# Where the transposes of a banded attention stand among the matrix products of a gated layer

## The chip, the cores and the metric

The kernel runs on one core of a Trainium2 chip. The metric is the device time of one execution in microseconds (us). The engines of a core work side by side, each through its own queue in order: TensorE (PE in the profile, with its weight loads as PEld), VectorE (DVE), ScalarE (ACT), GpSimd (POOL), and SyncE (SP), which issues the DMAs. They wait for each other by semaphores.

## The reference

```python
# q, k, v: (8, 8, 576, 64); window 32, dilation 4; heads 0-3 plain, heads 4-7 dilated
scores = scale * np.matmul(q, k.transpose(0, 1, 3, 2))
scores = np.where(masks, scores, -1000000000.0)      # 32 keys of each query are left
scores = scores - np.max(scores, axis=-1, keepdims=True)
attn = np.exp(scores)
attn = attn / (np.sum(attn, axis=-1, keepdims=True) + 1e-09)
x = np.matmul(attn, v)                               # then (4608 tokens, 512)
...
xn = x / rms * rms_g
g = xn @ w_gate
silu = g * (1.0 / (1.0 + np.exp(-g)))
val = xn @ w_val
out = silu * val @ w_out                             # (4608, 512), d_ff = 1536
```

## The kernel before, in words

**Units.** The 4608 tokens are worked on in 16 units of 288 tokens. A unit has two parts. The *attention* of a unit is 14 small pieces, called bursts here (burst 0 to burst 13): each is one block of queries against its band of keys, for two heads at once. The *layer* of a unit is the product with the gate weights, with the value weights and with the output weights, in 12 slices j of 128 of the 1536 columns. While TensorE works through the layer of one unit, the attention of the next unit is slipped in between; units are named here by their attention, so "unit 7" is the attention that runs beside the layer of unit 6.

**Ticks.** The order is written out by hand. The main loop (L747 to L775) goes through ticks, three for each slice j: in the gate tick `gate` runs the 12 products into PSUM tile `g` (L588 to L590: each 32-bit product is made of three products of split parts), in the value tick `val` runs 12 products into tile `v`, and in the output tick `proj` adds 12 products of an earlier slice into the four `acc` tiles. After the products of a tick, `attend` (L713) puts the attention steps of this tick behind them: the transposes of one burst, the output product of another, the scores of a third, in this order (L457). `plan` (L706) says at which ticks: a burst has its scores at tick q, its transposes five ticks later (L726), its output product eight ticks later. From the third unit's attention on the scores come every second tick, so that scores and output product share a tick, and the transposes stand in the ticks between.

**A burst, step by step.** Scores (L455) go to PSUM tile `s`. One tick later `scores_max` (L332, L337, DVE) takes them out, two ticks later `scores_exp` (L347, ACT) makes exponentials, four ticks later `scores_norm` (L350) sums and inverts on DVE (L354, L355) and multiplies on POOL, once for each of the two heads (L357). Then TensorE transposes the two 96 x 128 blocks of `t` into spare columns of a PSUM bank (L429), one tick later `untranspose` copies them out in two parts on ACT (L412) and DVE (L414), and the output product (L443, L444) reads these.

**Spare columns.** Tiles `g` and `v` have one bank of 512 columns each and use 288; the transposes get the next 192. `free` says whose: in the gate tick the gate's, in the value tick again the gate's (`g_free`, filled one tick earlier), in the output tick the value's (`v_free`). A tile is guarded as a whole: an instruction that writes spare columns waits for the readers of the 288 that stand ahead of it, and a reader waits for the writers ahead of it. The gate's readers are the hyperbolic tangent on ACT (L622) and `silu` on DVE (L627), both issued one tick after the gate tick; the value's reader is `prod` on DVE (L640), issued one tick after the value tick, which puts the slice's result together. Its split (L651 ACT, L652 POOL) is read three ticks later by `proj`.

**Order within a tick.** What other engines do in a tick is put off by `later` and written out by `flush` at the tick's start, in the order of a rank: `scores_norm` has -1, `prod` 0, `untranspose` 0.2, the copy of the output product (L377) 0.5, `scores_max` 0.7, `silu` 0.8, exponentials 2, the addition L387 4, the splits of q and k 3 to 5 (L315 on DVE, L306 on POOL).

Of the kernel before, what the change touches and what calls it, by code (L numbers as in the profile page):

```python
# [49 lines left out]
def geometry(u, c):  # L50


    half = u % 2
    if c < NC // 2:
        if half:
            return [(QB * i, QB * i, 0, P) for i in range(U // QB)], QB, U + W
        return [(QB * i, max(QB * i - W, 0), 0 if i else W, P if i else QB)
                for i in range(U // QB)], QB, U
    nq = U // DIL
    keys = nq + (W if half else 0)  # L60
    return [(nq * r, keys * r, 0 if half else W, keys) for r in range(DIL)], nq, keys * DIL
# [3 lines left out]
def attn_moe(ctx: ExitStack, tc: tile.TileContext, qk_in, v_in, w_gate, w_val, w_out, rms_g, outT):  # L65
# [41 lines left out]
    def later(dt, rank, fn):  # L107
        put_off.setdefault(now[0] + dt, []).append((rank, fn))

    def flush():  # L110
        for _, fn in sorted(put_off.pop(now[0], []), key=lambda e: e[0]):
            fn()
# [61 lines left out]
    def decode(k):  # L174

        for _ in range(k):
            later(0, 5, step)
# [20 lines left out]
    def split_weight(kind, j, e):  # L198
        n = pieces.index((kind, j))
        m, k = divmod(n, 2)  # L200

        tag = f"hi{n if n % 4 == 3 and n < 2 * NP - 4 else n - n % 4}"
        if tag not in his:
            parts = 1 if n % 4 == 3 and n < 2 * NP - 4 else 3 if n < 2 * NP - 4 else 4
            his[tag] = cst.tile([P, parts, NC, P], F32R, tag=tag, name=f"{tag}_{kind}{j}")
        hi = his[tag][:, 0 if tag == f"hi{n}" else n % 4]
        if k == 0:
            los[m] = cst.tile([P, 2, NC, P], F32R, tag=f"slot{state['free']}", name=f"lo_{m}")
        else:
            state["free"] = m  # L210
        lo = los[m][:, k]
        wts[kind, j] = hi, lo
        A.copy(out=hi, in_=single(kind, j))
        e.tensor_tensor(out=lo, in0=single(kind, j), in1=hi, op=ALU.subtract)
# [186 lines left out]
    def bursts(u):  # L401
        return [(u, c, i) for c in range(NC) for i in range(len(geometry(u, c)[0]))]
# [206 lines left out]
    def gate(u, j):  # L609
        g_ps = group("g", u, j)  # L610
        if u == 0:
            used.append(("g", j))
        g = g_ps[:, :U]

        def tanh():
            nonlocal g
            t = (sb.tile([P, U], F32, tag="hhi", name=f"h_{j}", bufs=2) if u == 0 else
                 sb.tile([P, U], F32, tag="th", name=f"th_{u}_{j}", bufs=1))
            if u + j == 0:
                g = sb.tile([P, U], F32, tag="hhi", name="g_first", bufs=2)  # L620
                V.tensor_tensor(out=g, in0=g_ps[:, :U], in1=root[0], op=ALU.mult)
            A.activation(out=t, in_=g, func=AF.Tanh, scale=0.5)  # L622
            gv[u, j] = t

        def silu():
            t = gv[u, j]
            V.scalar_tensor_tensor(out=t, in0=t, scalar=1.0, in1=g, op0=ALU.add, op1=ALU.mult)  # L627

        later(1, 0 if u + j else 0.65, tanh)
        later(1, 0.8, silu)  # L630
        return g_ps[:, U:U + 2 * QB]

    def val(u, j):
        v_ps = group("v", u, j)
        if u == 0:
            used.append(("v", j))

        def prod():
            t = gv[u, j]
            V.tensor_tensor(out=t, in0=t, in1=v_ps[:, :U], op=ALU.mult)  # L640
            if u + j == 0:
                V.tensor_tensor(out=t, in0=t, in1=root[0], op=ALU.mult)

        def parts():
            t = gv.pop((u, j))
            if u == 0:
                hs[u, j] = t
                return
            hi = sb.tile([P, U], F32R, tag="hhi", name=f"hhi_{u}_{j}", bufs=2)
            lo = late[0].tile([P, U], F32R, tag="hlo", name=f"hlo_{u}_{j}", bufs=2)  # L650
            A.copy(out=hi, in_=t)  # L651
            G.tensor_tensor(out=lo, in0=t, in1=hi, op=ALU.subtract)  # L652
            hs[u, j] = (hi, lo)

        later(1 if u + j else 2, 0, prod)
        later(1 if u + j else 2, 0.5, parts)
        return v_ps[:, U:U + 2 * QB]

    def proj(u, j):
        if u == 0:  # L660
            used.append(("o", j))
        h = hs.pop((u, j))
        for d in range(NC):
            if j == 0:
                acc[u, d] = ps.tile([P, 512], F32, tag=f"acc{d}", name=f"acc_{u}_{d}")[:, :U]
            three(acc[u, d], weight("o", u, j), d, h, j == 0, j == NJ - 1)
            if j == NJ - 1:
                later(1, 0.7, lambda d=d: give(u, d))
# [35 lines left out]
    events = {}  # L704

    def plan(u, base, q_at, t_at, o_at):  # L706
        for b, *ts in zip(bursts(u), q_at, t_at, o_at):
            for kind, t in zip("qto", ts):
                events.setdefault(base + t, {})[kind] = b
        events.setdefault(base + o_at[-1] + 3, {})["sum"] = u  # L710
        events.setdefault(base + o_at[-1] + (5 if u else 4), {})["apply"] = u

    def attend(t_ps, **tags):  # L713
        e = events.pop(now[0], {})
        if any(k in e for k in "qto"):
            products(e.get("q"), e.get("t"), e.get("o"), t_ps, **tags)
        if "sum" in e:
            rms_sum(e["sum"])
        if "apply" in e:
            rms_apply(e["apply"])  # L720

    ends = nb + LAG + OUT + 5
    plan(0, 0, range(nb), range(LAG, nb + LAG), range(LAG + OUT, nb + LAG + OUT))
    for u in range(1, NU):
        q_at = [LAST - (LAST - EARLY[u > NNAT]) * (nb - 1 - k) // (nb - 1) for k in range(nb)]
        t_at, o_at = [t + 5 for t in q_at], [t + 8 for t in q_at]  # L726
        if u < NNAT:
            q_at = (-1, 1, 2, 4, 5, 7, 8, 10, 11, 13, 14, 16, 17, 19)
            t_at, o_at = [t + 5 for t in q_at], [t + 7 for t in q_at]
        plan(u, ends - 2 + 3 * NJ * (u - 1), q_at, t_at, o_at)  # L730
    for n in range(ends):
# [10 lines left out]
        if n == ends - 1:  # L742
            _, v_free = gate(0, 0), val(0, 0)
# [3 lines left out]
    for u in range(NU):  # L747
        for j in range(NJ):
            for part in range(0 if u + j else 2, 3):
                t = 3 * (u * NJ + j) + part  # L750
                if used and (t % 3 != 2 if t >= SPLITS else t % 2 == 0):
                    later(0, 6, lambda: split_weight(*used.pop(0), V if t >= SPLITS else G))
                if u == 0:
                    decode(2 if t < 6 else 1 + t % 2 if len(ops) > 3 else int(t > 30))
                opening = len(ops) <= 3
                flush()
                if opening and not late:
                    early.close()
                    late.append(ctx.enter_context(tc.tile_pool(name="late", bufs=2)))
                if part == 0:  # L760
                    free = gate(u, j)
                elif part == 1:
                    free = val(u, j)
                else:
                    if prev is not None:
                        proj(*prev)
                    prev = (u, j)
                    free = v_free
                if part == 1:
                    g_free, v_free = g_free, free  # L770
                    free = g_free
                elif part == 0:
                    g_free = free
                attend(free)
                now[0] += 1  # L775
    flush()
# [69 lines left out]
```

## Time and profile before

| | us |
|---|---|
| median of three runs | 1160.24 (1160.02 to 1163.11) |
| the profiled execution's own time | 1162.36 |
| its span in the trace | 1160.6 |
| TensorE busy in the span | 1125.2 (97%) |
| VectorE, ScalarE, GpSimd busy | 798.8, 716.1, 611.5 |

The profiled execution lies 2.1 us above the median, and 1.8 us of it lie outside the traced span. In the trace a matmul's record is longer than the step to the next one, since matmuls are pipelined: the step from one 288-column product to the next is 0.13 us, the record 0.29 us. How late a matmul came is therefore read from start to start. The first 141 us hold the attention and the layer of the first unit, in another form (L585, L452, L438), and the stretch from 141 to 209 us the second unit's layer; after that each unit takes 67.5 us until the last, whose layer has no attention beside it.

### The profile page before, as it was taken

The page shows a single profiled execution, that of the slowest core. Times are in us where ns is not written, and L with a number is a line of the kernel's source. Part 1 is how long each engine was busy: PE and PEld are TensorE (multiplying, and loading weights), DVE is VectorE, ACT ScalarE, POOL GpSimd, SP SyncE. Part 2 cuts the span into 40 slices and gives each one's busy share as a digit, 9 for nine tenths or more (in the row PEclk, how much of TensorE's full clock was granted, in tenths as well). Part 3 has the DMA queues.
Part 4 walks back from the last instruction along what each step waited for, and adds up shares of the span by engine and source line. Part 5 has one row for each costly group of instructions (what it writes and reads, how often), then busy time and mean ns, then how long its engine had stood idle before and what let it go on. Part 6 is the DMA issues. An engine that isn't in the chain of part 4 may idle for free.

```text
span 1160.6 us, 25964 instructions
## 1 busy us (share of the span) xinstructions
PE 1125.2 (97%) x8357; PEld 1088.5 (94%) x8357; DVE 798.8 (69%) x2898; ACT 716.1 (62%) x2605; POOL 611.5 (53%) x1087
## 2 busy tenths in 40 slices
PE   8799788999999999999999999999999999999998
PEld 7577588999999999999999999999999999999998
DVE  5899777866758676675858767585776758586421
ACT  7476376675757567575666757576665757666311
POOL 6365344565546556564555655465565645565211
PEclk9899899999999999999999999999999999999999
DMA  8555221221213122131312213131221313120000
GB/s 245 156 210 179 76 75 39 80 61 31 82 37 103 39 70 62 35 86 34 95 41 81 58 31 90 31 101 40 71 61 35 95 33 91 38 81 15 1 21 22
DMA packets 61545, 82.19 MB, mean 71 GB/s; under 512 B 7298, under 2 KB 41090, under 8 KB 61410
## 3 DMA queue, kind: packets, MB, share of 16 engines
q1 hardware_dynamic: 61410, 80.54, 23.2%
q8 instruction: 67, 1.10, 0.4%
q14 instruction: 68, 0.56, 0.2%
HBM read 71.08 MB, written 9.44 MB: 69 GB/s over the span
## 4 chain that ended last, share of the span: by engine, by line
PE 75%; DVE 18%; issue 3%; ACT 2%; DMA 1%; POOL 0%; SPq 0%; POOLq 0%; DVEq 0%; ACTq 0%
PE acc L588 8%; PE acc L589 7%; PE acc L590 7%; PE g L588 7%; PE v L588 7%; PE g L590 7%; PE g L589 7%; PE v L589 7%; PE v L590 7%; DVE qs L315 3%; PE s L455 3%; PE o L443 3%; DVE t L337 2%; DVE xraw L551 2%; PE g L429 2%
## 5 line engine op out<-in xcount | busy, mean ns | idle before, releaser
L652 POOL TENSOR_TENSOR hlo<-th,hhi 128x288 fp32r<-128x288 f32 x180 | 144.8, 805 | 200.7 <-ACT hhi L651 196.9
L357 POOL TENSOR_SCALAR t<-t,sum 72x104 f32<-72x104 f32 (+3 forms) x442 | 165.7, 386 | 113.6 <-DVE sum L355 97.7
L590 PE MATMUL acc<-hhi,lo 128*128 128x288 f32 x720 | 212.1, 295 | 0.0
L590 PE MATMUL g<-xhi,lo 128*128 128x288 f32 x612 | 181.0, 296 | 0.0
L590 PE MATMUL v<-xhi,lo 128*128 128x288 f32 x612 | 180.3, 295 | 0.0
L651 ACT CAST hhi<-th 128x288 fp32r<-128x288 f32 x180 | 78.0, 433 | 163.7 <-DVE th L640 159.9
L347 ACT ACTIVATE t<-t,sum 96x128 f32<-96x128 f32 (+3 forms) x448 | 166.8, 375 | 12.3 <-DVE sum L337 11.4
L276 POOL TENSOR_TENSOR vlo<-vt,vhi 128x128 fp32r<-128x128 f32 x196 | 93.5, 477 | 122.7 <-ACT vhi L272 103.0
L387 DVE TENSOR_TENSOR xraw<-o,xraw 64x96 f32<-64x96 f32 (+1 forms) x392 | 106.8, 272 | 61.2 <-ACT xraw L377 56.4
L622 ACT ACTIVATE th<-g 128x288 f32<-128x288 f32 x180 | 73.8, 410 | 121.4 <-PE g L590 93.4
L590 PEld LDWEIGHTS acc<-hhi,lo 128*128 128x128 f32 x720 | 135.3, 188 | 0.0
L332 DVE TENSOR_TENSOR t<-s,mask 96x256 f32<-96x256 f32 (+3 forms) x196 | 71.7, 366 | 81.0 <-PE s L455 61.8
L627 DVE SCALAR_TENSOR_TENSOR th<-th,g 128x288 f32<-128x288 f32 x180 | 80.4, 447 | 68.0 <-ACT th L622 68.0
L590 PEld LDWEIGHTS g<-xhi,lo 128*128 128x128 f32 x612 | 115.5, 189 | 0.0
L590 PEld LDWEIGHTS v<-xhi,lo 128*128 128x128 f32 x612 | 115.1, 188 | 0.0
L588 PE MATMUL g<-xhi,hi_g 128*128 128x288 f32 x357 | 111.4, 312 | 0.6 <-DVE pt L414 0.5
L377 ACT COPY xraw<-o 64x96 f32<-64x96 f32 (+1 forms) x392 | 101.0, 258 | 16.1 <-PE o L444 13.8
L588 PE MATMUL acc<-hhi,hi_o 128*128 128x288 f32 x360 | 110.3, 306 | 0.0
L306 POOL TENSOR_TENSOR ks<-qk,ks 128x288 fp32r<-128x288 f32 (+2 forms) x112 | 107.4, 973 | 3.4 <-ACT ks L301 3.4
L589 PE MATMUL acc<-hlo,hi_o 128*128 128x288 f32 x360 | 106.6, 296 | 0.0
L640 DVE TENSOR_TENSOR th<-th,v 128x288 f32<-128x288 f32 x180 | 81.4, 452 | 36.2 <-PE v L590 33.2
L589 PE MATMUL g<-xlo,hi_g 128*128 128x288 f32 x322 | 95.4, 296 | 0.0
(173 smaller groups left out, 3569.7 us busy)
## 6 DMA issues: line engine op xcount, KB each, us to landing
qk<-in_qk_dram SPq DMA_DIRECT2D x60, 288.0 KB, 2.8
vt<-in_v_dram SPq DMA_DIRECT2D x196, 64.0 KB, 1.9
qk<-in_qk_dram SPq DMA_DIRECT2D x30, 352.0 KB, 3.0
out_dram<-ot SPq DMA_DIRECT2D x64, 144.0 KB, 1.9
qk<-in_qk_dram SPq DMA_DIRECT2D x30, 304.0 KB, 2.8
raw<-in_w_gate_dram SPq DMA_DIRECT2D x12, 512.0 KB, 4.3
raw<-in_w_val_dram SPq DMA_DIRECT2D x12, 512.0 KB, 4.0
raw<-in_w_out_dram SPq DMA_DIRECT2D x12, 512.0 KB, 4.2
```

The lines of the kernel that those rows point to most:

```text
L276: G.tensor_tensor(out=vl, in0=vs.pop(b), in1=vh, op=ALU.subtract)
L306: ek.tensor_tensor(out=ks[:, 1, :nkt], in0=kr, in1=ks[:, 0, :nkt], op=ALU.subtract)
L347: A.activation(out=t[:nq, a, :n], in_=t[:nq, a, :n], func=AF.Exp, scale=-1.0, bias=sm[:nq, a, 0:1], accum_out=sm[:nq, a, 1:2])
L357: (V if u == 0 and (c, i) > (NC - 1, 0) else G).tensor_scalar(out=t[:nq, a, :n], in0=t[:nq, a, :n], scalar1=sm[:nq, a, 3:4], scalar2=1.0, ...
L377: A.copy(out=to[a * D:(a + 1) * D], in_=o[a * D:(a + 1) * D, (2 + a) * nq:(3 + a) * nq])
L387: V.tensor_tensor(out=to[rows], in0=o[rows, a * nq:(a + 1) * nq], in1=to[rows], op=ALU.add)
L588: PE.matmul(out, wh[:, cc, :], xh, start=start, stop=False)
L589: PE.matmul(out, wh[:, cc, :], xl, start=False, stop=False)
L590: PE.matmul(out, wl[:, cc, :], xh, start=False, stop=stop)
L627: V.scalar_tensor_tensor(out=t, in0=t, scalar=1.0, in1=g, op0=ALU.add, op1=ALU.mult)
L640: V.tensor_tensor(out=t, in0=t, in1=v_ps[:, :U], op=ALU.mult)
L652: G.tensor_tensor(out=lo, in0=t, in1=hi, op=ALU.subtract)
```

## The change

Two edits. In `plan`, the transposes of every unit but the first that would stand in an output tick move to the value tick just ahead, unless that tick has transposes already. In the main loop, transposes in a value tick get the value's own spare columns, which the products just ahead have opened, in place of the gate's; those in a gate tick stay with the gate's, and the few left in an output tick with the value's.

```diff
     def plan(u, base, q_at, t_at, o_at):
+        t_at = [t - 1 if u and t % 3 == 2 and t - 1 not in t_at else t for t in t_at]
         for b, *ts in zip(bursts(u), q_at, t_at, o_at):
...
                 if part == 1:
-                    g_free, v_free = g_free, free
-                    free = g_free
-                elif part == 0:
-                    g_free = free
+                    v_free = free
                 attend(free)
```

With the scores every second tick this moves bursts 0, 3, 6, 9 and 12 of each unit from unit 3 on, and four bursts of unit 2: 69 in all. The second unit's transposes stand in gate and value ticks already and only change their bank.

The order on TensorE about burst 3 of unit 7, whose transposes read `t_7_1_0`. `v_6_0` and `g_6_1` are the products of the layer with value and gate, `o_7_0_1` and `s_7_1_2` the output product and the scores of other bursts. Before:

```order
L590 MATMUL v_6_0_6980<-xhi_6_3_6902,lo_0_621 128x288
L443 MATMUL o_7_0_1_6994<-pt_7_0_1_6895,vhi_1_1354 128x384
L444 MATMUL o_7_0_1_6994<-pt_7_0_1_6895,vlo_1_1355 128x192
L455 MATMUL s_7_1_2_6993<-ks_7_2_6691,qs_7_2_6726 96x256
...
L590 MATMUL acc_5_3_6044<-hhi_5_11_6898,lo_17_2226 128x288
L429 MATMUL v_6_0_6980<-ident_64,t_7_1_0_6868 128x96 x2
L588 MATMUL g_6_1_7051<-xhi_6_0_6810,hi0_g0_620 128x288
```

The same place after the change:

```order
L590 MATMUL v_6_0_6980<-xhi_6_3_6902,lo_0_621 128x288
L429 MATMUL v_6_0_6980<-ident_64,t_7_1_0_6868 128x96 x2
L443 MATMUL o_7_0_1_6994<-pt_7_0_1_6895,vhi_1_1354 128x384
L444 MATMUL o_7_0_1_6994<-pt_7_0_1_6895,vlo_1_1355 128x192
L455 MATMUL s_7_1_2_6993<-ks_7_2_6691,qs_7_2_6726 96x256
...
L590 MATMUL acc_5_3_6044<-hhi_5_11_6898,lo_17_2226 128x288
L588 MATMUL g_6_1_7051<-xhi_6_0_6815,hi0_g0_620 128x288
```

The two transposes moved past twelve products into `acc`, the output product and the scores; they are now the first thing behind the value's products.

The order on VectorE in the output tick that follows. `th_6_0` is the slice's result (`prod` at L640), `pt_7_1_0` the copy of the transposed burst 3, `sum2` belongs to `scores_norm` of burst 4. Before:

```order
L640 TENSOR_TENSOR th_6_0_6969<-th_6_0_6969,v_6_0_6980 128x288
L332 TENSOR_TENSOR t_7_1_2_7006<-s_7_1_2_6993,mask_77 96x256
...
L387 TENSOR_TENSOR xraw_7_0_6931<-o_7_0_1_6994,xraw_7_0_6931 64x96 x2
L354 TENSOR_REDUCE sum2_88<-sum2_88 96x2
L355 RECIPROCAL sum2_88<-sum2_88 96x2
L414 TENSOR_TENSOR pt_7_1_0_7034<-v_6_0_6980,pt_7_1_0_7034 128x192
```

After:

```order
L640 TENSOR_TENSOR th_6_0_6969<-th_6_0_6969,v_6_0_6980 128x288
L414 TENSOR_TENSOR pt_7_1_0_7002<-v_6_0_6980,pt_7_1_0_7002 128x192
L332 TENSOR_TENSOR t_7_1_2_7011<-s_7_1_2_6993,mask_77 96x256
...
L387 TENSOR_TENSOR xraw_7_0_6931<-o_7_0_1_6994,xraw_7_0_6931 64x96 x2
L354 TENSOR_REDUCE sum2_88<-sum2_88 96x2
L355 RECIPROCAL sum2_88<-sum2_88 96x2
```

The copy-out of the moved burst went one tick earlier with its transposes, ahead of `scores_max`; ACT's half (L412) moved in the same way. The order on POOL did not change at all, and neither did the place of `scores_norm` on DVE.

On TensorE the bursts that already stood in a value tick keep their place and change the bank, here burst 1 of unit 7, before:

```order
L589 MATMUL v_5_11_6875<-xlo_5_3_5812,hi32_g11_2153 128x288
L590 MATMUL v_5_11_6875<-spare_2444,lo_16_2154 128x288
L429 MATMUL g_5_11_6846<-ident_64,t_7_0_1_6750 128x96 x2
L588 MATMUL acc_5_0_6032<-hhi_5_10_6806,hi32_g11_2153 128x288
L589 MATMUL acc_5_0_6032<-hlo_5_10_6807,hi32_g11_2153 128x288
```

And after:

```order
L589 MATMUL v_5_11_6875<-xlo_5_3_5812,hi32_g11_2153 128x288
L590 MATMUL v_5_11_6875<-spare_2449,lo_16_2154 128x288
L429 MATMUL v_5_11_6875<-ident_64,t_7_0_1_6750 128x96 x2
L588 MATMUL acc_5_0_6032<-hhi_5_10_6811,hi32_g11_2153 128x288
L589 MATMUL acc_5_0_6032<-hlo_5_10_6812,hi32_g11_2153 128x288
```

Only the bank that the transposes write, `g_5_11` or `v_5_11`, differs.

## The prediction

> **What bounds the kernel now.** I read the busy times by stretch first. The columns are the stretch, its length, busy time and count for PE, PEld, DVE, ACT and POOL, the granted clock, the DMA share, GB/s.
>
> ```profile
> 44.00:110.00 66.00, 59.16 (x291) 46.38 (x292) 64.38 (x134) 46.00 (x130) 37.78 (x43) 0.97 0.53 186
> 110.00:141.00 31.00, 23.38 (x94) 17.57 (x93) 25.07 (x47) 13.74 (x37) 12.59 (x15) 0.89 0.23 72
> 173.00:209.00 36.00, 32.23 (x245) 30.81 (x244) 25.02 (x86) 23.70 (x80) 15.87 (x31) 1.00 0.13 35
> 344.00:1090.00 746.00, 743.43 (x5786) 737.85 (x5785) 519.79 (x2008) 481.95 (x1811) 418.54 (x759) 1.00 0.20 59
> ```
>
> In the long stretch PE is busy for 743.4 of 746.0 us, at full clock. DVE has the next most, 70%. So the time is the sum of PE's own steps and of whatever holds PE up: an edit that only reorders gains what PE waited before and pays what PE waits afterwards. From 44 to 110 us DVE is the bound (64.4 of 66.0).
>
> Next the waits of PE: engine, tile and line, who ended the wait, total us, times, longest.
>
> ```profile
> PE rps L495 <- DVE sq L399: 4.8, 1, 4.8
> PE v L429 <- DVE th L640: 3.6, 3, 1.8
> PE g L429 <- DVE h L627: 3.2, 2, 2.8
> PE g L429 <- DVE th L627: 1.7, 3, 1.2
> PE v L588 <- DVE pt L414: 1.0, 2, 0.8
> ```
>
> The transposes (L429) wait for `prod` (L640) and `silu` (L627), which don't make what they transpose: they read the other columns of the bank that the transposes are about to write.
>
> **What is removed: waits for the bank's other readers.** Burst 1 of each unit from unit 3 on stands in a value tick and uses the gate's bank. Here are the last product with the value and the transposes, in unit 7 and in unit 8.
>
> ```profile
> 488.81 0.30 PE L590 MATMUL v<-spare,lo 128*128 128x288 f32 x1
> 489.40 0.36 PE L429 MATMUL g<-ident,t 96*128 96x96 f32 x2 [0.29 <-DVE sum L354]
> ...
> 556.49 0.29 PE L590 MATMUL v<-xhi,lo 128*128 128x288 f32 x1
> 556.91 0.36 PE L429 MATMUL g<-ident,t 96*128 96x96 f32 x2
> ```
>
> Without a wait the next start comes 0.13 us later. So 0.46 us go in unit 7 and 0.29 in unit 8; odd units (7 of them, 3 to 15) and even ones (6, 4 to 14) look alike among themselves. In the value's own bank nothing has been read yet: 7 x 0.46 + 6 x 0.29 = 4.9 us gone.
>
> The L640 and L627 waits of 3.6 and 1.7 us, and the wait of the value's products for the copy-out (L414, 1.0), lie nearly all in unit 2, before 209 us: 6.3 us. That unit moves four bursts; at the odd unit's price worked out below (1.7 us) 4.6 are left. DVE and ACT have 25.0 and 23.7 of 36 us there, so PE, let go, soon meets the next late result: I take half, 2.3 us, with ends of 0 and 4.6. The 3.2 us on L627 in the first unit's layer I count at nothing: DVE fills 64.4 of 66 us there and hides them; were that cover gone, they would be 3.2 us more of gain.
>
> **What is added: a wait for the softmax's own result.** A burst's last multiplication on POOL (L357) is issued four ticks after its scores. A moved burst's transposes now stand in that same tick, right behind the products with the value, and PE takes its instructions in order. So I compared, for each moved burst, when POOL was done with when PE was through with those products, which is the start of what stands behind them now. PE for unit 7 (bursts 0, 3, 6, 9) and then unit 8 (bursts 0, 3, 6):
>
> ```profile
> 483.40 0.40 PE L455 MATMUL s<-ks,qs 128*96 128x256 f32 x2
> ...
> 495.08 0.34 PE L443 MATMUL o<-pt,vhi 128*128 128x384 f32 x1
> ...
> 506.72 0.33 PE L443 MATMUL o<-pt,vhi 128*128 128x384 f32 x1
> ...
> 518.18 0.30 PE L443 MATMUL o<-pt,vhi 104*128 104x288 f32 x1
> ...
> 551.13 0.40 PE L455 MATMUL s<-ks,qs 128*96 128x256 f32 x2
> ...
> 562.59 0.34 PE L443 MATMUL o<-pt,vhi 128*128 128x384 f32 x1
> ...
> 574.12 0.34 PE L443 MATMUL o<-pt,vhi 128*128 128x384 f32 x1
> ```
>
> POOL's multiplications of the same seven bursts, two heads in one row:
>
> ```profile
> 483.33 0.72 POOL L357 TENSOR_SCALAR t<-t,sum 96x128 f32<-96x128 f32 x2 [0.80 <-DVE sum L355]
> ...
> 495.13 0.71 POOL L357 TENSOR_SCALAR t<-t,sum 96x128 f32<-96x128 f32 x2 [0.79 <-DVE sum L355]
> ...
> 506.36 0.68 POOL L357 TENSOR_SCALAR t<-t,sum 72x104 f32<-72x104 f32 x2
> ...
> 516.97 0.67 POOL L357 TENSOR_SCALAR t<-t,sum 72x104 f32<-72x104 f32 x2
> ...
> 550.97 0.66 POOL L357 TENSOR_SCALAR t<-t,sum 96x96 f32<-96x96 f32 x2 [0.80 <-DVE sum L355]
> ...
> 562.09 0.66 POOL L357 TENSOR_SCALAR t<-t,sum 96x96 f32<-96x96 f32 x2 [0.79 <-DVE sum L355]
> ...
> 573.80 0.61 POOL L357 TENSOR_SCALAR t<-t,sum 72x72 f32<-72x72 f32 x2 [0.53 <-DVE sum L355]
> ```
>
> POOL ends late by 0.65, 0.76 and 0.32 us in unit 7 and by 0.50, 0.16 and 0.29 in unit 8; burst 9 is ready 0.54 us early, and burst 12 too. Before, these transposes came a whole tick later and never felt it. The sum: 7 x 1.73 + 6 x 0.95 = 17.8 us. Behind the waiting transposes on PE are queued the output product, the scores and everything after; behind `prod`, which now has to wait for the transposes too, stands all of DVE's tick.
>
> Does the chain come earlier or later than before? For burst 3 of unit 7, DVE's steps from the previous scores to the sums (first two rows), the split of q for bursts 0 of unit 7 and 3 of unit 8 (next two), and POOL's split of k beside the first:
>
> ```profile
> 492.00 0.42 DVE L332 TENSOR_TENSOR t<-s,mask 96x256 f32<-96x256 f32 x1 [0.28 <-PE s L455]
> ...
> 492.99 1.03 DVE L315 TENSOR_TENSOR qs<-qk,qs 64x288 fp32r<-64x288 f32 x1
> ...
> 481.13 1.71 DVE L315 TENSOR_TENSOR qs<-qk,qs 64x288 fp32r<-64x288 f32 x1
> ...
> 560.48 0.49 DVE L315 TENSOR_TENSOR qs<-qk,qs 64x288 fp32r<-64x288 f32 x1
> ...
> 491.36 2.35 POOL L306 TENSOR_TENSOR ks<-qk,ks 128x416 fp32r<-128x416 f32 x2
> ```
>
> The chain begins with PE's scores (the bracket), so a PE that is late makes it late by the same: a new wait doesn't pay itself back one period on. But the split of q takes 0.49 us alone and 1.03 or 1.71 while POOL splits k, and PE, held up at burst 0 by 0.65 us and freed of 0.46 at burst 1, shifts the two against each other. For burst 3 of odd units I take off half of 1.03 - 0.49: 7 x 0.27 = 1.9 us, with ends of 0 and 3.8. Remaining: 15.9 us. An arrival may cost up to 0.1 us more where the weights can't be loaded ahead: 39 x 0.1 = 3.9 us, kept for the range.
>
> **What is moved.** The copy-out of a moved burst (L414, ACT's L412) goes one tick earlier, ahead of `scores_max`. DVE has the same work in the two ticks together as before; what is delayed by up to a copy, 0.36 us, are the sums of the next burst, here burst 4 of unit 7: the copy, POOL's multiplication and the transposes.
>
> ```profile
> 495.00 0.36 DVE L414 TENSOR_TENSOR pt<-g,pt 128x192 fp32r<-128x192 f32 x1
> ...
> 498.66 0.72 POOL L357 TENSOR_SCALAR t<-t,sum 96x128 f32<-96x128 f32 x2
> ...
> 501.07 0.28 PE L429 MATMUL g<-ident,t 96*128 96x96 f32 x1
> ```
>
> POOL is done at 499.38, 1.7 us ahead of the transposes: price nothing. Were that cover gone, it would be 0.36 us a time. No DMA, and nothing on POOL or SP, changes place.
>
> A run of small matmuls also costs a change-over. Transposes alone between two groups of products:
>
> ```profile
> 601.95 0.30 PE L590 MATMUL v<-xhi,lo 128*128 128x288 f32 x1
> 602.08 0.29 PE L429 MATMUL g<-ident,t 72*72 72x72 f32 x2
> 602.17 0.38 PE L588 MATMUL acc<-hhi,hi_g 128*128 128x288 f32 x1
> 602.39 0.29 PE L589 MATMUL acc<-hlo,hi_g 128*128 128x288 f32 x1
> ```
>
> From 601.95 to 602.39 are 0.44 us where two steps take 0.26: 0.18 us, of which 0.09 are the transposes themselves and 0.09 a late next product. Joined to an output product and scores the 0.09 may be saved or not, since the output product also has to load weights behind two short matmuls. I take 0.03: 69 x 0.03 = 2 us saved, with ends of 0 and 69 x 0.09 = 6.2. The Trainium skill, "TensorE: Matmul & The Clock Gate", section on what each phase is for, says that weight loads are pulled ahead of running matmuls, so that they overlap. By that rule the late next product would not be there, and joining would save nothing: the sum would be 2 us higher. The row with its 0.22 us step to 602.39 speaks against it here.
>
> **The sum.** +15.9 - 4.9 - 2.3 - 2.0 = +6.7 us. The rows come from an execution of 1162.36 us with a span of 1160.6; on the median of 1160.24 this gives 1166.9 us. With the ends: 14.0 - 4.9 - 4.6 - 6.2 = -1.7, and 17.8 + 3.9 - 4.9 = +16.8: 1158.5 to 1177.0.
>
> **Rivals.**
> - *The splits no longer collide, and it gets faster.* If PE's shift frees the split of q of POOL at bursts 0 and 3, the sums come up to 1.2 and 0.5 us earlier: burst 0 no longer waits, burst 3 of odd units by 0.22. Left are 7 x (0.22 + 0.32) + 6 x (0.16 + 0.29) = 6.5 us; with unit 2's gain in full, 6.5 - 4.9 - 4.6 - 2.0 = -5.0: 1155.2 us. It decides from new waits below 5.7 us on (4.9 + 2.3 + 2.0 less 3.5). For it speaks how much L315 varies; against it, that at burst 0 both splits follow from the same PE step, and that at burst 6 of unit 7 POOL itself is the queue. Chance 0.14.
> - *New waits and old ones cancel.* The engines use PE's halts to run ahead, and half of the 17.8 remain: 8.9 - 4.9 - 2.3 - 2.0 = -0.3, 1159.9 us. Against it: the chain starts from PE's scores. Chance 0.20.
> - *The halts cost clock as well.* The stretch with the 4.8 us wait was granted 0.89 over 31 us, 3.4 us lost. If each of the 39 halts cost half of that, 1.7 us, it would be 66 us on top: 1233 us. The stretch from 173 to 209 us, at 1.00, has this halt in it:
>
> ```profile
> 185.66 0.29 PE L429 MATMUL v<-ident,t 72*72 72x72 f32 x2 [1.83 <-DVE th L640]
> ```
>
>  Ours are below 0.8 us. The Trainium skill, same page, section on psum-queue depth-cycling, tells of short idle times between groups of matmuls that let the clock swing; this row doesn't bear it out. Chance 0.02.
>
> That the change might not do what it says is excluded by the order on the engines.
>
> **Chances.** My forecast, waits for the softmax that outweigh those removed, has 0.64. About 0.3% (3.5 us) is what a measurement of this kernel can tell from no change. Slower 0.66 (with the clock rival), same 0.20, faster 0.14. The range takes the forecast's ends and the cancelling case: 1157 to 1177 us; the faster rival's point and the clock rival lie outside.
>
> **What would show it.** In the changed kernel's profile L429 should wait for POOL L357 some 39 times in all, at bursts 0, 3 and 6, for 12 to 20 us; the waits on L640 and L627 should be nearly gone after 209 us; beside an odd unit's attention the layer should take 0.85 us longer (1.73 - 0.27 - 0.46 - 5 x 0.03), beside an even one's 0.5 (0.95 - 0.29 - 0.15). I am wrong if POOL is ready in time (the L315 rows near 0.5 us at bursts 0 and 3), or if the waits are there and the units are no longer for it.

## The result, and the profile after

| | before | after |
|---|---|---|
| median, us | 1161.67 (4 runs, 1160.02 to 1165.05) | 1183.04 (4 runs, 1181.50 to 1183.22) |
| ratio | 1 | 1.0171 [1.0153, 1.0189] |
| profiled execution, us | 1162.36 | 1181.50 |
| its span, us | 1160.6 | 1179.7 |

The changed kernel is slower by 1.7%, by 19.1 us in the span. The direction was forecast, the size was not: 6.7 us were worked out, and the range ended at 1177 us.

The first line is the page's busy times of after. The second fence is the view by stretch, of the same four stretches as in the prediction and with the same columns.

```profile
PE 1134.1 (96%) x8357; PEld 1088.5 (92%) x8357; DVE 796.8 (68%) x2898; ACT 708.1 (60%) x2605; POOL 616.8 (52%) x1087
```

```profile
44.00:110.00 66.00, 59.12 (x291) 47.11 (x292) 61.45 (x136) 45.88 (x131) 41.90 (x43) 0.97 0.55 192
110.00:141.00 31.00, 23.84 (x100) 18.06 (x99) 24.98 (x49) 13.88 (x39) 13.66 (x15) 0.89 0.24 77
173.00:209.00 36.00, 32.92 (x250) 31.63 (x249) 25.87 (x88) 24.26 (x84) 17.08 (x33) 1.00 0.12 35
344.00:1090.00 746.00, 735.96 (x5656) 722.38 (x5656) 515.26 (x1991) 469.18 (x1789) 411.79 (x748) 1.00 0.20 59
```

In the long stretch PE got through 5656 matmuls where it had got through 5786, and is idle for 10.0 us instead of 2.6. The clock is 1.00 there as before, and in each of the other stretches it is what it was: no time went to the clock.

Where the 19.1 us lie can be read from the first products of each layer. The second unit's layer, which runs from 141.5 to 221.6 us in before, starts 1.4 us earlier in after; it takes the same 80.1 us; the thirteen layers behind it, beside the attention of units 3 to 15, take 20.5 us longer together (beside an odd unit 1.7 on average, beside an even one 1.4); the tail is equal. So the whole loss is in the steady units.

Who holds PE up, from the list of PE's waits in after:

```profile
PE v L429 <- POOL t L357: 14.0, 30, 2.3
```

The wait on POOL is new and heads the list; those on L640 and L627 are gone. The list understates it: it counts only the time in which no record of PE runs, and a matmul's record (0.29 us) outlasts its step (0.13). Here are the transposes of unit 7 in after (bursts 0, 1, 3, 6 and 9), each behind the last product with the value:

```profile
488.54 0.29 PE L590 MATMUL v<-spare,lo 128*128 128x288 f32 x1
489.03 0.65 PE L429 MATMUL v<-ident,t 96*128 96x96 f32 x2 [0.20 <-POOL t L357]
...
494.65 0.30 PE L590 MATMUL v<-spare,lo 128*128 128x288 f32 x1
494.79 0.33 PE L429 MATMUL v<-ident,t 96*128 96x96 f32 x2
...
500.30 0.29 PE L590 MATMUL v<-xhi,lo 128*128 128x288 f32 x1
501.39 0.65 PE L429 MATMUL v<-ident,t 96*128 96x96 f32 x2 [0.80 <-POOL t L357]
...
513.16 0.29 PE L590 MATMUL v<-xhi,lo 128*128 128x288 f32 x1
513.62 0.60 PE L429 MATMUL v<-ident,t 72*104 72x72 f32 x2 [0.17 <-POOL t L357]
...
525.19 0.29 PE L590 MATMUL v<-xhi,lo 128*128 128x288 f32 x1
525.33 0.29 PE L429 MATMUL v<-ident,t 72*104 72x72 f32 x2
```

And POOL's multiplications of bursts 0, 3, 6 and 9 of unit 7:

```profile
488.60 0.72 POOL L357 TENSOR_SCALAR t<-t,sum 96x128 f32<-96x128 f32 x2 [0.80 <-DVE sum L355]
...
500.97 0.72 POOL L357 TENSOR_SCALAR t<-t,sum 96x128 f32<-96x128 f32 x2 [0.79 <-DVE sum L355]
...
513.22 0.68 POOL L357 TENSOR_SCALAR t<-t,sum 72x104 f32<-72x104 f32 x2
...
524.39 0.68 POOL L357 TENSOR_SCALAR t<-t,sum 72x104 f32<-72x104 f32 x2
```

Read as in the prediction, POOL's end against the product's start plus a step of 0.13. Burst 0: 489.32 against 488.67, late by 0.65. Burst 3: 501.69 against 500.43, late by 1.26. Burst 6: 513.90 against 513.29, late by 0.61. Burst 9: 525.07 against 525.32, ready. Burst 1's transposes start 0.14 us behind the product: their old wait is gone.

On PE, from start to start (the first transpose against the product plus a step, the second against the first plus its step without a wait, 0.07 to 0.09 us), the moved transposes of the thirteen units wait 26.4 us. Burst 0 was forecast exactly (0.65), bursts 3 and 6 came out at 1.26 and 0.61 where 0.76 and 0.32 stood. The account of the thirteen layers, in which 38 of the 39 waits lie:

| term, us | forecast | measured in the trace |
|---|---|---|
| waits for POOL at bursts 0, 3, 6 | +15.9 | +25.7 |
| next matmul starts 0.10 us behind a transpose that waited, not 0.03 | 0 (3.9 kept for the range) | +2.8 |
| burst 1 no longer waits | -4.9 | -4.7 |
| other old waits gone: bursts 4, 7 and 10 on the gate's bank (1.8), the value's products on burst 0's copy-out (1.1) | not in the sum | -2.9 |
| transposes joined with other small matmuls | -2.0 | -0.4 (what is left over) |
| sum | +9.0 | +20.5 |

### The profile page after: what moved, and what is told of

Same layout as the page of the kernel before. It is cut to its first block, busy times and chain, and to the rows that moved or that the text cites. A ratio compares the mean times of both kernels' runs of the same rounds, so it can differ in the third digit from the quotient of the medians.

```text
span 1179.7 us, 26024 instructions
## 1 busy us (share of the span) xinstructions
PE 1134.1 (96%) x8357; PEld 1088.5 (92%) x8357; DVE 796.8 (68%) x2898; ACT 708.1 (60%) x2605; POOL 616.8 (52%) x1087
## 4 chain that ended last, share of the span: by engine, by line
PE 68%; DVE 18%; ACT 7%; issue 3%; POOL 3%; DMA 1%; SPq 0%; POOLq 0%; DVEq 0%; ACTq 0%
PE acc L588 7%; PE acc L589 7%; PE acc L590 7%; PE g L588 6%; PE g L589 6%; PE g L590 6%; PE v L588 6%; PE v L590 5%; PE v L589 5%; DVE qs L315 3%; PE s L455 3%; PE o L443 2%; PE v L429 2%; DVE t L337 2%; DVE t L332 2%
## 5 line engine op out<-in xcount | busy, mean ns | idle before, releaser
L357 POOL TENSOR_SCALAR t<-t,sum 72x104 f32<-72x104 f32 (+3 forms) x442 | 169.3, 395 | 116.2 <-DVE sum L355 108.2
L347 ACT ACTIVATE t<-t,sum 96x128 f32<-96x128 f32 (+3 forms) x448 | 166.8, 375 | 17.8 <-DVE sum L337 17.0
L412 ACT CAST pt<-v 128x192 fp32r<-128x192 f32 (+3 forms) x140 | 41.2, 294 | 190.9 <-DVE th L640 159.4
L627 DVE SCALAR_TENSOR_TENSOR th<-th,g 128x288 f32<-128x288 f32 x180 | 80.4, 447 | 67.1 <-ACT th L622 67.0
L640 DVE TENSOR_TENSOR th<-th,v 128x288 f32<-128x288 f32 x180 | 81.5, 453 | 41.7 <-PE v L590 22.3
L588 PE MATMUL g<-xhi,hi_g 128*128 128x288 f32 x357 | 106.3, 298 | 0.0
```

The costliest lines, as they stand in the source:

```text
L347: A.activation(out=t[:nq, a, :n], in_=t[:nq, a, :n], func=AF.Exp, scale=-1.0, bias=sm[:nq, a, 0:1], accum_out=sm[:nq, a, 1:2])
L357: (V if u == 0 and (c, i) > (NC - 1, 0) else G).tensor_scalar(out=t[:nq, a, :n], in0=t[:nq, a, :n], scalar1=sm[:nq, a, 3:4], scalar2=1.0, ...
L588: PE.matmul(out, wh[:, cc, :], xh, start=start, stop=False)
```

## The experiments

Theory 1: the loss is the moved transposes' wait for the softmax, larger at burst 3 than forecast because PE, freed at burst 1, arrives earlier there while the softmax does not. Theory 2: sharing the value's bank is dear in itself, because the copy-out by ACT then has to wait until `prod` on DVE has read the bank. Theory 3: the copy-outs, a tick earlier, delay DVE. The ratios below are to the kernel before, timed on the same chip. "Twelve layers" are those beside the attention of units 4 to 15, from the first gate product of the first to that behind the last: 808.4 us before, 827.0 after.

### The bank alone

```diff
-        t_at = [t - 1 if u and t % 3 == 2 and t - 1 not in t_at else t for t in t_at]
```

> The bank edit alone: transposes in a value tick go to the value's own bank, none moves a tick earlier. Theory 1 (the loss is all in the moved transposes, which wait for the softmax; their wait at burst 3 grew because burst 1 no longer holds PE up): no wait on POOL, the 4.9 us at burst 1 and some 2 us of unit 2 gone, so about 7 us faster than before, ratio 0.994. Theory 2 (sharing the value's bank is dear by itself: ACT's copy-out now waits for VectorE's product of the slice, and this delays the splits behind it): the gain is eaten, 0 to 3 us slower, ratio 1.000 to 1.003. Theory 3 (the copy-out that goes a tick earlier delays VectorE): as theory 1, since nothing goes earlier here.

Measured: 1158.11 us, 0.9953 [0.9936, 0.9970]. Twelve layers take 804.4 us, 4.0 less than before, and from 209 us on the list of PE's waits is empty. The long stretch:

```profile
344.00:1090.00 746.00, 745.80 (x5818) 742.96 (x5817) 527.41 (x2014) 477.94 (x1812) 420.14 (x759) 1.00 0.20 59
```

PE is busy for all but 0.2 us. This half of the change is a gain, of nearly the size that burst 1's waits had; theory 2, as a loss by itself, falls. But POOL's result for burst 3 comes later here, though no transposes moved. The last product of the value tick in which the move would put burst 3 of unit 5, and POOL's multiplication:

```profile
358.61 0.29 PE L590 MATMUL v<-xhi,lo 128*128 128x288 f32 x1
...
359.33 0.71 POOL L357 TENSOR_SCALAR t<-t,sum 96x128 f32<-96x128 f32 x2 [0.79 <-DVE sum L355]
```

POOL ends at 360.04, 1.30 us behind the products' end at 358.74; in before it was 0.76 in the same unit. No transpose waits for it in this kernel.

### The move alone

Before, with the line in `plan` and nothing else, so that the moved transposes write the gate's bank:

```diff
+        t_at = [t - 1 if u and t % 3 == 2 and t - 1 not in t_at else t for t in t_at]
```

> The move alone: the same 69 transposes stand a tick earlier, but value ticks use the gate's bank as before. Theory 1: burst 1 keeps its wait of 0.46 (odd units) and 0.29 us, so burst 3 waits only as worked out from the trace of before, 0.76 and 0.16; all waits 17.8 us, plus 3 us of weights loaded late, less 6 us of joined runs: 15 us slower than before, ratio 1.013. Theory 2: also about 15 us, since no copy-out shares the value's bank. Theory 3: burst 3 waits 1.2 us in odd units as in the changed kernel, 22 to 24 us slower, ratio 1.020.

Measured: 1178.56 us, 1.0131 [1.0115, 1.0147]. Burst 3 of unit 7:

```profile
498.29 0.29 PE L590 MATMUL v<-xhi,lo 128*128 128x288 f32 x1
499.16 0.35 PE L429 MATMUL g<-ident,t 96*128 96x96 f32 x2 [0.57 <-POOL t L357]
```

The transposes start 0.74 us behind the products' end at 498.42: burst 3 waits about what was forecast. Theory 3, which had 1.020, falls. Theory 1 has the right time here, but not for its reason, since burst 1 hardly waits: 0.15 us in odd units and not at all in even ones, as here in unit 8:

```profile
561.68 0.30 PE L590 MATMUL v<-xhi,lo 128*128 128x288 f32 x1
561.83 0.35 PE L429 MATMUL g<-ident,t 96*128 96x96 f32 x2
```

In its place the moved transposes also wait for the gate's reader `silu` (L627 ends 4.6 us of PE's waits from 209 us on). So PE is free at burst 1 of the even units, and burst 3 still waits only 0.27 us there, not 0.6 as in after. And 1.0131 - 1 and 0.9953 - 1 add up to 1.0084, not to 1.0171: the two halves make each other worse by some 0.9%, about 10 us.

### Burst 1 back in the gate's bank

```diff
                 if part == 1:
                     v_free = free
+                    t = events.get(now[0], {}).get("t")
+                    if t and t[0] > NNAT and t[1:] == (0, 1):
+                        free = g_free
+                elif part == 0:
+                    g_free = free
```

> The changed kernel with burst 1 of each unit from unit 3 on put back into the gate's bank. Theory 1: burst 1 waits again (0.46 and 0.29 us) and burst 3 waits that much less; the time is that of the changed kernel within 2 us, ratio to before 1.016 to 1.018. Theory 2: the other bursts still share the value's bank, the waits at burst 3 stay at 1.2 and 0.6 us and burst 1's 4.9 us come on top: ratio 1.021. Theory 3: as theory 2.

Measured: 1181.17 us, 1.0154 [1.0136, 1.0172]. Bursts 1 and 3 of unit 7:

```profile
497.18 0.29 PE L590 MATMUL v<-spare,lo 128*128 128x288 f32 x1
497.68 0.36 PE L429 MATMUL g<-ident,t 96*128 96x96 f32 x2 [0.21 <-DVE sum L354]
...
503.23 0.29 PE L590 MATMUL v<-xhi,lo 128*128 128x288 f32 x1
503.83 0.65 PE L429 MATMUL v<-ident,t 96*128 96x96 f32 x2 [0.30 <-POOL t L357]
```

In after, burst 3's pair began 0.96 us behind the products' end (501.39 - 500.43), here 0.47 (503.83 - 503.36): 0.49 us less, where burst 1 waits 0.37 more. Over the units burst 1 waits 4.5 us again, and burst 3 5.7 instead of 11.6. The time barely moves: what a wait at burst 1 costs, burst 3 gives back. That is what theory 1 says, but this kernel also takes burst 1's copy-out out of the value's bank; it doesn't tell which of the two counts.

### Burst 4 back in the gate's bank

The same edit for burst 4, `t[1:] == (1, 1)`, to find what makes burst 6 late.

> The changed kernel with burst 4 of each unit from unit 3 on put back into the gate's bank. It tests where the extra wait at burst 6 comes from (0.66 and 0.6 us in place of 0.32 and 0.29), since burst 4 did not wait before. If ACT's copy-out of burst 4, which in the value's bank waits for VectorE's product, delays the splits: burst 6 waits 0.3 us less, some 4 us off the changed kernel, ratio 1.0135. If it comes from PE running ahead or from the copy-outs that moved: no change, 1.017.

Measured: 1179.28 us, 1.0143 [1.0123, 1.0163]. Burst 6 of unit 8, here and then in after:

```profile
579.63 0.29 PE L590 MATMUL v<-xhi,lo 128*128 128x288 f32 x1
579.82 0.55 PE L429 MATMUL v<-ident,t 72*72 72x72 f32 x2
```

```profile
581.88 0.29 PE L590 MATMUL v<-xhi,lo 128*128 128x288 f32 x1
582.28 0.55 PE L429 MATMUL v<-ident,t 72*72 72x72 f32 x2
```

The step is 0.19 us here and 0.40 in after. Burst 6's waits fall from 7.7 to 6.0 us in all. In ten of the thirteen units POOL is late by 0.3 us, as in before; in three it is late by 1.0 to 1.3, for a reason that wasn't looked into. So a copy-out of burst 4 from the value's bank does hold the chain up: theory 2 has a part after all.

### Both back

Bursts 1 and 4, `t[1:] in ((0, 1), (1, 1))`.

> The changed kernel with bursts 1 and 4 of each unit from unit 3 on back in the gate's bank, so that only the moved transposes write the value's bank in a value tick. If the two causes found for the larger waits are all there is (burst 1's wait comes back at burst 3; burst 4's copy-out delays burst 6), the waits are those worked out from the trace of before: transposes late by 0.65, 0.76 and 0.32 us in odd units, 0.50, 0.16 and 0.29 in even ones, burst 1 by 0.46 and 0.29, and the time is burst 4's with burst 1 changed for burst 3: 16 us slower than before, ratio 1.0135. If something else of the change is at work, waits at bursts 3 and 6 stay larger by 0.2 us or more, ratio from 1.015 on.

Measured: 1179.95 us, 1.0155 [1.0139, 1.0171], span 1176.1. Bursts 3 and 6 of unit 7 on PE, POOL's multiplications for them, and DVE's steps ahead of the first:

```profile
499.27 0.29 PE L590 MATMUL v<-xhi,lo 128*128 128x288 f32 x1
499.87 0.65 PE L429 MATMUL v<-ident,t 96*128 96x96 f32 x2 [0.30 <-POOL t L357]
...
511.67 0.29 PE L590 MATMUL v<-xhi,lo 128*128 128x288 f32 x1
511.87 0.60 PE L429 MATMUL v<-ident,t 72*104 72x72 f32 x2
```

```profile
499.44 0.72 POOL L357 TENSOR_SCALAR t<-t,sum 96x128 f32<-96x128 f32 x2 [0.79 <-DVE sum L355]
...
511.47 0.68 POOL L357 TENSOR_SCALAR t<-t,sum 72x104 f32<-72x104 f32 x2
```

```profile
496.31 0.42 DVE L332 TENSOR_TENSOR t<-s,mask 96x256 f32<-96x256 f32 x1 [0.28 <-PE s L455]
...
497.31 1.02 DVE L315 TENSOR_TENSOR qs<-qk,qs 64x288 fp32r<-64x288 f32 x1
```

POOL ends late by 0.76 at burst 3 (500.16 against 499.40) and by 0.35 at burst 6 (512.15 against 511.80): the figures of the trace of before. All waits of the moved transposes sum to 17.5 us, where 17.8 was worked out. So the sum of the waits was right for a kernel in which bursts 1 and 4 stay as they were, and what those two add is 26.4 - 17.5 = 8.9 us. The span is 3.6 us shorter than that of after; by the spans the ratio is 1.0134, as expected; the timed one is 0.002 above, which isn't explained.

### The softmax a tick earlier

```diff
-            later(3 if q[0] < NNAT else 4, -1, lambda: scores_norm(*q))
+            later(3, -1, lambda: scores_norm(*q))
```

> The changed kernel with the softmax's sums and POOL's multiplication (L350) written out one tick earlier, three ticks after the scores. All three theories hold the wait for POOL to be the loss: it should vanish from the list of PE's waits, 27 to 30 us less than the changed kernel, so some 9 us faster than before, ratio 0.992. If the transposes cost by standing in the value's bank or behind its products, whatever they wait for, it stays near 1.017; if VectorE or ACT now comes late with something else, in between, and the list of waits names it.

Measured: 1195.95 us, 1.0277 [1.0253, 1.0300], far from the 0.992 expected. PE's waits, then the one of DVE's that is new in size (3.4 us in after):

```profile
PE s L455 <- DVE sum L337: 15.7, 14, 2.4
PE o L443 <- DVE xraw L387: 10.6, 17, 1.1
```

```profile
DVE sum L354 <- ACT t L347: 57.5, 73, 2.0
```

PE no longer waits for POOL, but at the head of the tick the sums stand in front of all that DVE has to do, and they wait there for ACT's exponentials. What PE needs from DVE comes late instead.

### The softmax a tick earlier, in mid-tick

The same line with rank 0.75 from the third unit on, behind `scores_max`.

> The changed kernel with the softmax's sums and POOL's multiplication written out three ticks after the scores, but behind the maxima of that tick, so that VectorE doesn't come to them before ACT's exponentials are through (as it did, for 57.5 us, when they stood first). Theory 1: no wait on POOL and none on ACT in its place, 28 us less than the changed kernel: ratio 0.992. If the waits on VectorE's additions and maxima come back all the same, the loss belongs to VectorE's load in these ticks and not to the late sums: ratio above 1.005.

Measured: 1169.85 us, 1.0053 [1.0037, 1.0069]. First of PE's waits:

```profile
PE o L443 <- DVE xraw L387: 9.1, 10, 1.6
```

The moved transposes now wait 0.4 us in all in place of 26.4, and the twelve layers take 809.5 us, 17.5 less than after. So the wait on POOL is the bulk of the loss. It is not 0.992, since DVE's additions are late in turn, and unit 2 takes 5.5 us longer than in after, for a reason that wasn't looked into.

### The moved transposes last in their tick

```diff
-        parts = [(b, fn, a) for b, fn in ((t, transposed), (o, output), (q, scored)) for a in range(2)]
+        steps = ((t, transposed), (o, output), (q, scored))
+        if t and t[0] >= NNAT:
+            steps = steps[1:] + steps[:1]
+        parts = [(b, fn, a) for b, fn in steps for a in range(2)]
```

> The changed kernel, but in a tick that has several attention steps the transposes stand behind the output product and the scores, not ahead of them. Theory 1 (the time is the wait for POOL): this work, 0.44 us with an output product and 0.23 at burst 0, which has scores alone, covers part of each wait: of 26.8 us of waits from unit 3 on about 12 are left, so 15 us less than the changed kernel, ratio 1.004. If the place directly behind the products with the value or the joined run is what costs, it stays near 1.017.

Measured: 1170.38 us, 1.0067 [1.0052, 1.0082]; the span is 12.5 us shorter than that of after. Burst 3 of unit 7:

```profile
494.93 0.40 PE L455 MATMUL s<-ks,qs 128*96 128x256 f32 x2
495.20 0.30 PE L429 MATMUL v<-ident,t 96*128 96x96 f32 x1
495.82 0.30 PE L429 MATMUL v<-ident,t 96*128 96x96 f32 x1 [0.32 <-POOL t L357]
```

The first transpose is ready; the second, for the other head, still comes 0.62 us behind it, since POOL multiplies the heads one after the other. The output product and the scores in front hide a part of the wait, not all, which is the likely reason for the 0.003 above what was expected.

### Only bursts 9 and 12 moved

```diff
-        t_at = [t - 1 if u and t % 3 == 2 and t - 1 not in t_at else t for t in t_at]
+        t_at = [t - 1 if u and t > 10 and t % 3 == 2 and t - 1 not in t_at else t for t in t_at]
```

> The bank edit with the move only for bursts 9 and 12 (in unit 2 for its last two), whose result POOL has ready 0.3 to 0.8 us before the products with the value end. Theory 1: no wait on POOL, and 27 joined runs that save 0.09 us each: 2 to 3 us below the bank edit alone, ratio to before 0.993. If a move costs by itself, by the copy-out that goes earlier on ACT and VectorE or by the joined run, it comes out at or above the bank edit's 0.995.

Measured: 1157.06 us, 0.9947 [0.9934, 0.9960], the fastest kernel here, though not to be told from the bank alone (0.9953). The bursts that were forecast not to wait do not. This trace gives the worth of joining without a wait, measured from the last product ahead to the third one behind, less three steps of 0.1325, at the same places and so with the same shapes as in the trace of before. Burst 9's transposes with output product and scores take 0.57 us, where apart they take 0.40 and 0.18; burst 12's with an output product alone 0.42, where apart they take 0.24 and 0.18. Joining saves nothing to speak of.

### The move the other way

The moved bursts one tick later, into the gate tick and the gate's bank:

```diff
-        t_at = [t - 1 if u and t % 3 == 2 and t - 1 not in t_at else t for t in t_at]
+        t_at = [t + 1 if u and t % 3 == 2 and t + 1 not in t_at else t for t in t_at]
```

> The bank edit with the same transposes moved the other way: one tick later, behind the products with the gate and in the gate's own bank, instead of one tick earlier. Theory 1 (what costs is the softmax that comes too late for an earlier place; the joined run itself is a gain): no wait for POOL, the waits on the bank's readers gone as in the bank edit, and 65 joined runs; at 0.09 us each, as measured at bursts 9 and 12 of the changed kernel, 6 us below the bank edit, ratio to before 0.990; at the 0.02 us that the late bursts alone showed, 0.994. If the joined run costs (copy-outs that meet the output product a tick later, the hyperbolic tangent behind the transposes), above 0.995.

Measured: 1164.34 us, 1.0009 [0.9997, 1.0020], where theory 1 had 0.990 to 0.994. There is no wait on POOL, but among PE's waits stands

```profile
PE o L443 <- DVE xraw L387: 5.8, 10, 1.4
```

and joining saves nothing here either: burst 9's three steps take 0.57 us, as behind the value's products. Against the bank alone, the thirteen steady layers take 4.7 us more and unit 2 3.9.

## Why the prediction was right or wrong

**Right: what is added.** PE was the bound, and the transposes moved in front of their own data. Bursts 0, 3 and 6 of each unit wait for POOL's multiplication, 39 times; bursts 9 and 12 do not. Moving only those two costs nothing, and giving POOL's result a tick earlier takes the waits away (26.4 to 0.4 us).

**Right, as far as it goes: what is removed.** Burst 1's 4.9 us (the two terms add up to 5.0) were there to gain: 4.8 in before, none in after. Another 2.9 us of old waits went that the sum had at nothing. They are short and hidden under PE's records: the transposes of bursts 4, 7 and 10 on the gate's bank, and the value's products behind burst 0's copy-out.

**Wrong: "Does the chain come earlier or later than before?"** This step took 1.9 us off the 17.8 for a split of q that might no longer collide; instead the waits grew to 26.4. It read POOL's lateness from the trace of before, in which bursts 1 and 4 still use the gate's bank. The same reading, POOL's end against the end of the products ahead, summed over the thirteen units in each kernel's own trace (the second transpose's own step is not taken off here, so that after's 27.5 us stand for the 26.4 us of PE's waits):

| kernel | burst 0 | burst 3 | burst 6 | sum, us |
|---|---|---|---|---|
| before | 7.5 | 6.2 | 4.5 | 18.2 |
| the move alone | 7.5 | 6.4 | 4.5 | 18.3 |
| the bank alone | 7.5 | 11.7 | 9.5 | 28.8 |
| after | 7.6 | 12.0 | 7.9 | 27.5 |
| burst 1 back in the gate's bank | 7.5 | 6.1 | 8.2 | 21.8 |
| burst 4 back | 7.5 | 11.4 | 6.2 | 25.1 |
| both back | 7.7 | 6.9 | 4.0 | 18.6 |

The growth comes with the bank and not with the move: at burst 3 with the bank of burst 1, at burst 6 with that of burst 4. The prediction's reason to expect no growth was "the chain begins with PE's scores", read from one bracket in the trace of before (`scores_max` at 492.00, 0.28 us idle, ended by PE). The steps of the same chain in after, on DVE, on ACT and on POOL, and ACT's copy-out of burst 1 in before:

```profile
495.19 0.43 DVE L640 TENSOR_TENSOR th<-th,v 128x288 f32<-128x288 f32 x1
...
497.48 0.41 DVE L332 TENSOR_TENSOR t<-s,mask 96x256 f32<-96x256 f32 x1
...
498.46 1.39 DVE L315 TENSOR_TENSOR qs<-qk,qs 64x288 fp32r<-64x288 f32 x1
```

```profile
495.65 0.32 ACT L412 CAST pt<-v 128x192 fp32r<-128x192 f32 x1 [1.00 <-DVE th L640]
```

```profile
497.20 2.34 POOL L306 TENSOR_TENSOR ks<-qk,ks 128x416 fp32r<-128x416 f32 x2
```

```profile
489.80 0.32 ACT L412 CAST pt<-g 128x192 fp32r<-128x192 f32 x1 [0.95 <-PE g L429]
```

Count from the last product ahead of burst 1's transposes, 488.81 in before and 494.65 in after. The transposes start 0.45 us earlier in after, and `scores_max` 0.36 us earlier: that part of the chain does follow PE. ACT's copy-out does not (0.99 and 1.00), and neither does POOL's split of k (2.55 in both), which stands behind the split of the slice's result and so behind the copy-out. And the split of q, though it starts 0.37 us earlier, again ends 0.31 us behind the split of k. So the sums and POOL's multiplication come when they came before, and what PE gained at burst 1 it waits at burst 3. The move alone is the test of it: PE is as free at burst 1 of the even units, but the copy-out begins 0.54 us behind the product in place of 0.99, and the lateness at burst 3 hardly grows (0.21 us for 0.15). With both bursts back in the gate's bank, the bracket, the 1.02 us of the split and the 0.76 us at burst 3 are all back.

What holds the copy-out is a part of the step that was left out: the prediction saw only that in the value's bank nothing has been read *yet*. The copy-out reads that bank later, on ACT, and so does `prod` on DVE, and the tile's guard puts one behind the other. The list of ACT's waits in after, then in before:

```profile
ACT pt L412 <- DVE th L640: 159.4, 123, 2.2
```

```profile
ACT hhi L651 <- DVE th L640: 159.9, 140, 2.5
...
ACT pt L412 <- PE g L429: 45.5, 56, 1.1
```

ACT waited for `prod` in before as well, but with the split of the slice's result; the copy-out of a burst from the gate's bank began as soon as PE had written. Now the copy-out stands behind `prod`, and so does everything after it, POOL's splits too. The Trainium skill, "PSUM — Partial Sum Buffer", section on bank collisions, says that two engines may not be at the same part of one bank at once, reads against reads included, and that software has to guard by bank; the row at 495.65, idle for 1.00 us until `prod`, agrees with such a guard. Of the 8.9 us, some 5 lie at burst 3 and some 3.8 at burst 6 (sums of the waits in after less those with both bursts back).

The rival in which the splits no longer collide came true in one odd unit of seven. In all seven the split of q starts within 0.01 us of POOL's second split of k. In the last unit it goes first and takes 0.45 us, and POOL's is the longer one; in the other six it takes 1.39 to 1.41 us where it had taken 1.03 to 1.06. The Trainium skill, "SBUF — State Buffer", section on the two sides of SBUF, has DVE and GpSimd share a port pair that one of them holds for a whole instruction; the traces agree (0.45 us when first, else an end 0.31 to 0.32 us behind POOL's).

**Mis-sized: weights that can't be loaded ahead.** The 3.9 us kept for the range are in part real: the matmul behind a transpose that waited starts 0.10 us after it, against 0.03 without a wait, 2.9 us over the 39. They belonged in the sum.

**Mis-sized: joined runs.** The term of 2.0 us measures nothing at bursts 9 and 12, place by place, and 0.4 us as what is left over of the account. The late matmul doesn't go away by joining, it moves: in after, at burst 9, the second part of the output product starts 0.21 us behind the first, where it was 0.13.

**Wrong: unit 2.** Half of the 4.6 us were expected back; the old waits are indeed gone from the list, and unit 2 takes the same 80.1 us. Others of the same sum stand there instead: 2.5 us on POOL's multiplication, 2.0 on a copy-out, 2.8 on scores and output products. The first unit's layer, counted at nothing, ended 1.4 us earlier, but that is no gain shown: up to there this kernel and the three with burst 1, burst 4 or both back are the same program, and the second unit's layer starts between 139.9 and 143.5 us in their traces.

**Rivals.** No clock was lost to 39 halts of up to 1.3 us. That old and new waits cancel is refuted: the waits left are 26.4 us and not 8.9.

## What to carry to other kernels

When a change has two halves, how early an operand is ready must be read from a trace that has the other half in it: here the bank alone, itself a gain, shows some 28 us of lateness, which the move then pays for. A wait on an engine that works in order also keeps it in step with the engines that feed it: before counting its removal as a gain, ask which queue sets the next operand, and if that is not this engine, expect the wait at the next operand instead. A bank has later readers too: ask who copies out, and behind whom. Moving work ahead is worth it only where its operand is already done, piece by piece: here it is for the two last bursts of five, and the change's other half alone is faster than both kernels.

## What the runs showed of the hardware

A matmul that waited for a semaphore costs more than its wait: the next one starts 0.10 us after it in place of 0.03 (all 39 times in after). A list of idle times hid two thirds of a wait on PE (9.4 us listed from 209 us on, 26.4 start to start), since the records of pipelined matmuls cover the first 0.16 us of each gap. And of two subtractions with both inputs in SBUF, on VectorE and on GpSimd, the one that starts second ends behind the first: where both start within 0.01 us of each other, VectorE's takes 0.45 us or 1.4 us.
